# Forming P-Q on VectorE in 54 pair steps of an FNet and squared-ReLU kernel

## The chip, the cores and the metric

The kernel runs on one core of a Trainium2 chip. The metric is the device time of one execution in microseconds (us). Shown for the kernel before are three runs: 633.65, 633.65 and 635.58 us, median 633.65. One execution was profiled; all durations and waits below are of that one.

TensorE (PE in the profile) multiplies matrices into PSUM, ScalarE (ACT) and VectorE (DVE) work element by element, GpSimd (POOL) issues the loads here, and SyncE (SP) issues the stores. Each engine takes its instructions in the order in which the program gives them, and waits on semaphores for the others.

## What is computed

The input x is 8 batches of 3008 tokens with 256 features. The reference takes the real part of a Fourier transform over tokens and features, and passes each token through a two-layer network without biases:

```python
X = np.fft.fft(np.fft.fft(x, axis=1), axis=2).real     # 8 x 3008 x 256
x = X.reshape(24064, 256)
h = np.maximum(x @ w_in, 0.0)                          # w_in 256 x 2048
out = (h * h) @ w_out                                  # w_out 2048 x 256
```

## The kernel before

The transform is real in and real out, so tokens come in pairs k and S-k. The kernel holds, for a column (one token of a pair), the cosine part zc and the sine part zs, 128 features each. The feature transform is folded into the weights w_in once: gh[:, 0] takes zc, gh[:, 1] takes zs. With P = gh0' zc and Q = gh1' zs, the hidden layer of token k is P+Q and that of its partner P-Q. There is one exception: row 0 of gh1 and zs carries the term of the highest feature frequency, whose sign does not turn. gh[:, 2] is therefore -2 gh1 with row 0 set to 0 (`turn2`, `gh_turn`, L448), so that adding gh2' zs to P+Q gives the partner.

**Windows.** The columns of all batches are cut into 25 windows (`wins`): six of 240 to 512 columns, windows 6 to 23 of 512 columns, and a last one of 360. One window is eight pair steps (`for s0 in range(0, NST, ng)`), each for 256 of the 2048 hidden features (two halves a of 128):

- `pq`: four passes on TensorE (L684, L685) form P+Q of 256 features x 512 columns in a PSUM tile ph of two banks (ps_h has two such tiles).
- `square(s, 0)`: ScalarE evicts ph through Relu to h1 (L694, f16, three buffers), VectorE squares h1 into h2 (L696).
- `others(s)`: what else is due in this step, below.
- `turn`: two passes (L690) add gh2' zs to the same ph, which then holds P-Q.
- `square(s, 1)`: the same eviction and square for the partner. It writes the columns in reversed order.

**What lies in `others`.** First the jobs `at[s]`, then sixteen matmuls of the second layer of the window before (`ffn2_steps`, L596: h2 x wout16), every second step followed by the eviction osb (L611) and its output stores on SP's queue (L576); then `post[s]`; then matmuls of the transform (z, L478) for the next window, with their evictions on ScalarE (es L483, zc and zs L487) and combinations on VectorE (L494).

**Folds.** In some windows `at` brings the folding of a later batch on VectorE: d_even (L348, L349, L350) in step 0, n_cos (L358) in step 1, d_odd (fo, L353) in step 2, which also triggers the load of the next batch on GpSimd (L125, L130), n_sin (L361) in step 3, odds (od, L368) in step 4, nyq in `post[5]`, even (L379) in step 6, and back in step 7 (writes ev to DRAM and reads it back as rb on GpSimd's queue, L381, L389, L391). nyq is two small matmuls py on TensorE (L373, L374) that read od, and a copy back into od on VectorE (L375). Of the windows from 6 on, 8, 10, 13, 16 and 19 have folds. Windows 6, 9, 12, 15, 18 and 21 have the second part of a fold on VectorE instead ("late": xt L404, yt L415, steps 2 to 5).

The order on each engine is the order of the program text: `tc.manual_schedule()`; nothing is reordered. Tiles of one tag share their buffers in turn.

Of the kernel before, what the change touches and what calls it, by code (L numbers as in the profile page):

```python
# [8 lines left out]
F32 = mybir.dt.float32  # L9
F16 = mybir.dt.float16  # L10
I32 = mybir.dt.int32
AF = mybir.ActivationFunctionType
ALU = mybir.AluOpType

HS = 32.0
P = 128
# [3 lines left out]
def rev_dim(ap, i):  # L20

    dims = [list(d) for d in ap.ap]
    step, cnt = dims[i]
    dims[i] = [-step, cnt]
    return bass.AP(tensor=ap.tensor, offset=ap.offset + step * (cnt - 1), ap=dims)
# [3 lines left out]
def kernel(  # L29
# [14 lines left out]
    nc = tc.nc  # L44
    B, S, D = x.shape
    _, F = moe_w_in.shape
# [7 lines left out]
    NFC = F // P  # L54
    WN = 512

    FIRST = [240, 512, 376, 376, 512, 448]
    R23 = float(2.0 ** 23)

    RQ = (1, 3, 5, 0, 2, 4)  # L60

# [11 lines left out]
    wins = []  # L73
# [5 lines left out]
    NW = len(wins)  # L79

    def win_of(col):
        return max(w for w in range(NW) if wins[w][0] <= col) if col < TOT else NW
# [17 lines left out]
    const = ctx.enter_context(tc.tile_pool(name="const", bufs=1))  # L100
    tmp = ctx.enter_context(tc.tile_pool(name="tmp", bufs=2))
# [7 lines left out]
    drp = ctx.enter_context(tc.tile_pool(name="drp", bufs=2, space=bass.MemoryType.DRAM))  # L109
    ps_h = ctx.enter_context(tc.tile_pool(name="ps_h", bufs=2, space=bass.MemoryType.PSUM))  # L110
    ps_o = ctx.enter_context(tc.tile_pool(name="ps_o", bufs=2, space=bass.MemoryType.PSUM))
# [56 lines left out]
    perm = [const.tile([P, P], F16, name=f"perm{i}") for i in range(2)]  # L168
# [3 lines left out]
    nc.gpsimd.memset(idx["c"][0:2, :], P - 3)  # L172
    idx["f"] = iota([P, 1], [[1, 1]], -1, 1, "idx_f")
    nc.gpsimd.memset(idx["f"][0:1, :], 0)
    w16 = [const.tile([P, 2, F // 2], F16, name=f"w16_{i}") for i in range(2)]
    for i in range(2):
        nc.gpsimd.dma_start(out=w16[i], in_=moe_w_in[:, i * F // 2 : (i + 1) * F // 2].rearrange("(c p) f -> p c f", p=P))
    wout16 = const.tile([P, NFC, D], F16, name="wout16")
# [2 lines left out]
    def small(shape, name):  # L181
        return const.tile(shape, F32, name=name)
# [22 lines left out]
    def table_steps(e):  # L205
# [19 lines left out]
        def args(h):  # L225
            t = st["t", h] = tmp.tile([P, 3, NE], F32, name="t", tag="tt")
            for j in range(nr):
                r = row(h, j)
                if e == 0:
                    nc.scalar.activation(t[:, j, 0:n], st["kf"], AF.Copy, bias=R23, scale=vs[:, r : r + 1])  # L230
                else:
                    nc.vector.tensor_scalar(out=t[:, j, 0:n], in0=st["kf"], scalar1=vs[:, r : r + 1], scalar2=R23, op0=ALU.mult, op1=ALU.add)

        def turns(h):
            t = st["t", h]
            nc.vector.tensor_scalar(out=t[:, 0:nr, 0:n], in0=t[:, 0:nr, 0:n], scalar1=-R23, scalar2=-float(S), op0=ALU.add, op1=ALU.mult)

# [44 lines left out]
    at = const.tile([P, 2, P + 1], F32, name="at")  # L282
    for c in range(2):
        nc.scalar.activation(at[:, c, :], drow, AF.Copy, bias=R23, scale=dvs[:, c : c + 1])
    nc.vector.tensor_scalar(out=at, in0=at, scalar1=-R23, scalar2=-float(D), op0=ALU.add, op1=ALU.mult)
    for c in range(2):
# [141 lines left out]
    gh = const.tile([P, 3, F], F16, name="gh")  # L428
# [17 lines left out]
    def gh_turn(cc):  # L446
        f0 = cc * 512
        nc.vector.tensor_scalar(out=gh[:, 2, f0 : f0 + 512], in0=gh[:, 1, f0 : f0 + 512], scalar1=turn2[:, 0:1], scalar2=None, op0=ALU.mult)  # L448
# [3 lines left out]
    def zwin(w):  # L452
        if w not in zc:
            zc[w] = zp.tile([P, WN], F16, name="zc", tag="zc")
            zs[w] = zp.tile([P, WN], F16, name="zs", tag="zs")
        return zc[w], zs[w]
# [101 lines left out]
    for cc in range(1, F // 512):  # L558
        gh_turn(cc)

    def store(osb, p0, g0, m, minus, eng=nc.sync):

        for b, k0, kstep, n, c0 in runs:
            il, ih = max(g0, c0) - c0, min(g0 + m, c0 + n) - 1 - c0
            if minus and k0 in (0, H):
                il = max(il, 1)
            cnt = ih - il + 1
            if cnt <= 0:
                continue
            if minus:  # L570
                lo = p0 + (m - 1) - (c0 + ih - g0)
                row = b * S + S - (k0 + kstep * ih)
            else:
                lo = p0 + c0 + il - g0
                row = b * S + k0 + kstep * il
            eng.dma_start(  # L576
                out=bass.AP(tensor=out.tensor, offset=out.offset + row * D, ap=[[kstep * D, cnt], [1, D]]),
                in_=osb[lo : lo + cnt, :])
# [51 lines left out]
    def fold_jobs(i):  # L630
        f = folds[i] = fold_steps(i)
        return [f["d_even"], f["n_cos"], f["d_odd"], f["n_sin"], f["odds"], f["nyq"], f["even"], f["back"]]

    fold_at, late_at = {}, {}
    for i in range(2, B):
        fold_at[win_of(col_of[i, 0]) - 2] = i
        late_at[win_of(col_of[i, 1]) - 2] = i
    NST = NFC // 2
    old = None
    for w in range(NW):  # L640
        g0, wn = wins[w]
        h2 = h2p.tile([P, NFC, 2 * WN], F16, name="h2", tag="h2")
        zcw, zsw = zwin(w)

        lo, hi = 0, NST - 1
        at = [[] for _ in range(NST)]
        post = [[] for _ in range(NST)]
        if w == 0:
            at[2] = [f0s["even"], f0s["back"]]
        elif w == 1:  # L650
            fj = fold_jobs(1)
            at = [[f] for f in fj[0:5]] + [[], [], []]
            post[5] = fj[5:6]
            lo, hi = 6, 7
        elif w == 2:
            te = table_steps(1)
            at = [[folds[1]["even"], lambda: te["freq"](), lambda: te["args"](0)], [lambda: te["turns"](0)], [lambda: te["mods"](0)],
                  [lambda: te["absm"](0)], [lambda: te["sins"](0)], [lambda: te["coss"](0)], [], [lambda: te["weigh"]()]]
            for st in range(4):
                at[st + 3] = at[st + 3] + f0s["late"][st : st + 1]  # L660
            at[7].append(folds[1]["back"])
        elif w in fold_at:
            fj = fold_jobs(fold_at[w])
            at = [[f] for f in fj[0:5]] + [[], fj[6:7], fj[7:8]]
            post[5] = fj[5:6]
        elif w == win_of(col_of[1, 1]) - 1:
            for st in range(4):
                at[st] = folds[1]["late"][st : st + 1]
            lo = 4
        if w in late_at:  # L670
            for st in range(4):
                at[st + 2] = at[st + 2] + folds[late_at[w]]["late"][st : st + 1]
        zj, zl = [], []
        for u in need[w + 1]:
            zu = z_steps(u)
            zj += [(zu, 0, 0), (zu, 1, 0), (zu, 0, 1), (zu, 1, 1)]
        f2 = ffn2_steps(*old) if old else []
        phs = {}

        def pq(s):  # L680
            ph = phs[s] = ps_h.tile([P, 2, 512], F32, name="ph", tag="psh")
            for a in range(2):
                f0 = (2 * s + a) * P
                nc.tensor.matmul(ph[:, a, 0:wn], gh[:, 0, f0 : f0 + P], zcw[:, 0:wn], start=True, stop=False)  # L684
                nc.tensor.matmul(ph[:, a, 0:wn], gh[:, 1, f0 : f0 + P], zsw[:, 0:wn], start=False, stop=True)  # L685

        def turn(s):
            for a in range(2):
                f0 = (2 * s + a) * P
                nc.tensor.matmul(phs[s][:, a, 0:wn], gh[:, 2, f0 : f0 + P], zsw[:, 0:wn], start=False, stop=True, skip_group_check=True)  # L690

        def square(s, sg):
            h1 = h1p.tile([P, 2, 512], F16, name="h1", tag="h1")
            nc.scalar.activation(h1[:, :, 0:wn], phs[s][:, :, 0:wn], AF.Relu)  # L694
            hv = rev_dim(h1[:, :, 0:wn], 2) if sg else h1[:, :, 0:wn]
            nc.vector.tensor_tensor(h2[:, 2 * s : 2 * s + 2, sg * wn : (sg + 1) * wn], hv, hv, op=ALU.mult)  # L696

        def others(s):
            for j in at[s]:
                j()  # L700
            for j in spread(f2, s, NST):
                j()
            for j in post[s]:
                j()
            if s == lo:
                zl[:] = [j for zu, part, h in zj for j in zu(part, h)]
            if s >= lo:
                for j in spread(zl, s - lo, hi - lo) if s < hi else []:
                    j()


        ng = 2 if w == 0 or wins[w - 1][1] < 384 < wn else 1
        for s0 in range(0, NST, ng):
            ss = range(s0, s0 + ng)
            for s in ss:
                pq(s)
            for s in ss:
                square(s, 0)
            others(s0)
            for s in ss:  # L720
                turn(s)
            for s in ss:
                square(s, 1)
            for s in ss[1:]:
                others(s)
        old = (w, h2)
    for j in ffn2_steps(*old, tail=True):
        j()
# [30 lines left out]
```

## Time and profile before

| what | value |
|---|---|
| median of the runs | 633.65 us |
| profiled execution, span from first to last instruction | 632.0 us |
| TensorE busy | 615.9 us, 97% |
| ScalarE busy | 457.4 us, 72% |
| VectorE busy | 369.5 us, 58% |
| GpSimd busy | 76.5 us, 12% |
| granted TensorE clock, share of full speed | 1.000 |
| second-layer matmuls L596 | 3024, 51% of the chain of waits |
| passes L684, L685, L690 | 400 each, 12% of the chain each |
| a pair step of a window of 512, no z matmuls | 3.04 us |

The span is what the profiler saw between the first and the last instruction; the run's time is 1.65 us more at the median. "Busy" of TensorE counts a matmul until it has drained, so neighbours overlap, and its mean duration (379 ns for a pass of 512 columns) is longer than the distance from one to the next. The distance is what counts for time; it is read from the timeline. In lines of groups and of the timeline, out<-in names the tiles, and what stands in brackets is the idle time of the engine before the instruction with what ended it.

### The profile page before, as it was taken

How to read it: one execution, taken by the hardware profiler on the slowest of the kernel's cores; microseconds unless marked ns; L12 is line 12 of the kernel's file. 1: busy time of each engine (PE TensorE's matmuls, PEld its weight loads, DVE VectorE, ACT ScalarE, POOL GpSimd, SP SyncE). 2: the span in 40 equal slices, each digit the busy share in tenths (PEclk: the TensorE clock that was granted, in tenths of full speed). 3: DMA queues.
4: the chain of work that ended last, by engine and by line, in shares of the span. 5: the costliest groups of instructions: out<-in, count | busy, mean ns of one | idle time of the engine just before them, and what ended most of it. 6: DMA issues, size and time to landing. Idle time of an engine off the chain costs nothing.

```text
span 632.0 us, 11586 instructions
## 1 busy us (share of the span) xinstructions
PE 615.9 (97%) x4548; PEld 439.1 (69%) x4548; DVE 369.5 (58%) x604; ACT 457.4 (72%) x610; POOL 76.5 (12%) x125
## 2 busy tenths in 40 slices
PE   5899999999999999999999999999999999999997
PEld 2457776776777767767777677777677776777786
DVE  7887656765457557645576455854557555454430
ACT  7787778777777677767777777777777777777662
POOL 5352200022002200220011100030000200000000
PEclk9999999999999999999999999999999999999999
DMA  8936211172112711631127211262111311111112
GB/s 146 211 82 127 85 34 34 50 164 78 36 43 58 184 46 42 144 97 35 51 44 160 74 52 39 59 151 73 40 31 55 111 34 47 38 46 35 49 54 65
DMA packets 36525, 47.52 MB, mean 75 GB/s; under 512 B 4216, under 2 KB 30328, under 8 KB 36472
## 3 DMA queue, kind: packets, MB, share of 16 engines
q0 software_dynamic: 9344, 22.14, 17.6%
q1 hardware_dynamic: 26899, 24.44, 12.7%
q8 instruction: 35, 0.57, 0.4%
q10 hardware_dynamic: 228, 0.21, 0.1%
q14 instruction: 19, 0.15, 0.1%
HBM read 33.63 MB, written 27.84 MB: 97 GB/s over the span
## 4 chain that ended last, share of the span: by engine, by line
PE 93%; DVE 3%; ACT 2%; issue 1%; POOL 0%; ACTq 0%; POOLq 0%; DVEq 0%
PE po L596 51%; PE ph L684 12%; PE ph L685 12%; PE ph L690 12%; PE pz L478 4%; ACT h L694 1%; PE pw L301 1%; DVE h L696 1%; PE pg L436 0%; ACT cos L259 0%; DVE fe L349 0%; DVE fo L353 0%; ACT sin L248 0%; ACT gh L440 0%; DVE od L368 0%
## 5 line engine op out<-in xcount | busy, mean ns | idle before, releaser
L694 ACT ACTIVATE h<-ph 128x1024 f16<-128x1024 f32 (+4 forms) x400 | 368.4, 974 | 80.0 <-PE ph L690 72.1
L696 DVE TENSOR_TENSOR h<-h 128x1024 f16<-128x1024 f16 (+4 forms) x400 | 262.4, 660 | 231.6 <-ACT h L694 228.2
L596 PE MATMUL po<-wout,h 128*128 128x256 f16 (+1 forms) x3024 | 361.6, 273 | 0.0
L596 PEld LDWEIGHTS <-h 128*128 128x128 f16 (+1 forms) x3024 | 296.8, 98 | 71.3
L684 PE MATMUL ph<-zc,gh 128*128 128x512 f16 (+4 forms) x400 | 145.9, 366 | 1.1 <-ACT h L694 0.8
L685 PE MATMUL ph<-zs,gh 128*128 128x512 f16 (+4 forms) x400 | 145.9, 366 | 0.4 <-ACT zs L487 0.4
L690 PE MATMUL ph<-zs,gh 128*128 128x512 f16 (+4 forms) x400 | 112.8, 366 | 2.0 <-ACT h L694 1.5
L611 ACT ACTIVATE osb<-po 128x512 f32<-128x512 f32 (+3 forms) x95 | 54.9, 582 | 57.4 <-PE po L596 52.4
L685 PEld LDWEIGHTS <-gh 128*128 128x128 f16 x400 | 39.1, 98 | 43.8 <-issue 2.5
L684 PEld LDWEIGHTS <-gh 128*128 128x128 f16 x400 | 39.0, 98 | 41.8 <-issue 0.5
L690 PEld LDWEIGHTS <-gh 128*128 128x128 f16 x400 | 37.2, 97 | 12.7 <-issue 4.3
L421 POOL COPY xt<-xt 128x2 f16<-128x2 f16 x16 | 2.5, 186 | 173.2 <-DVE xt L404 173.2
L130 POOL DMA_INDIRECT xo<-in_x_dram,idx_r x15 | 22.1, 1471 | 4.6 <-issue 4.6
L125 POOL DMA_DIRECT2D xo<-in_x_dram x8 | 6.0, 751 | 109.8 <-DVE fo L353 109.8
L483 ACT ACTIVATE es<-pz 128x376 f32<-128x376 f32 (+1 forms) x32 | 15.4, 481 | 5.3 <-PE pz L478 5.2
L391 POOL DMA_INDIRECT rb<-scr,idx_r x16 | 18.5, 1158 | 4.9 <-issue 4.9
L487 ACT ACTIVATE zs<-pz 128x376 f16<-128x376 f32 (+23 forms) x27 | 8.5, 358 | 9.9 <-PE pz L478 9.9
L349 DVE TENSOR_TENSOR fe<-xo 128x3072 f16<-128x3072 f16 x8 | 14.3, 1786 | 1.6 <-DMA xo<-in_x_dram,idx_r 1.3
L353 DVE TENSOR_TENSOR fo<-xo 128x3072 f16<-128x3072 f16 x8 | 14.2, 1779 | 0.0
L494 DVE SCALAR_TENSOR_TENSOR zc<-es,pz 128x376 f16<-128x376 f32 (+20 forms) x26 | 9.4, 392 | 7.2 <-ACT zc L487 7.0
L301 PE MATMUL pw<-spn 128*128 128x384 f16 x30 | 8.2, 448 | 5.2 <-DVE spn L290 5.2
L389 POOL DMA_DIRECT2D rb<-scr x16 | 8.8, 551 | 33.4 <-DMA scr<-ev 33.0
(106 smaller groups left out, 220.4 us busy)
## 6 DMA issues: line engine op xcount, KB each, us to landing
out_dram<-osb SPq DMA_DIRECT2D x77, 128.0 KB
xo<-in_x_dram POOLq DMA_DIRECT2D x7, 768.0 KB, 7.0
scr<-ev POOLq DMA_DIRECT2D x8, 390.0 KB, 4.4
rb<-scr POOLq DMA_DIRECT2D x16, 130.0 KB, 5.1
out_dram<-osb SPq DMA_DIRECT2D x12, 94.0 KB
w<-in_moe_w_in_dram POOLq DMA_DIRECT2D x2, 512.0 KB, 10.0
wout<-in_moe_w_out_dram POOLq DMA_DIRECT2D x1, 1024.0 KB, 14.5
out_dram<-osb SPq DMA_DIRECT2D x8, 75.0 KB
```

The source lines that it names most:

```text
L130: nc.gpsimd.indirect_dma_start(out=flat(q), out_offset=None, in_=bass.AP(tensor=x.tensor, offset=0, ap=[[XW, B * S * D // XW], [1, XW]]), ...
L301: nc.tensor.matmul(pw[:, 0 : 3 * P], spn[:, 0, 0, :], spn.rearrange("p c r d -> p (c r d)")[:, 0 : 3 * P], start=True, stop=True)
L391: nc.gpsimd.indirect_dma_start(out=rb[:, q].rearrange("p r d -> p (r d)"), out_offset=None, in_=bass.AP(tensor=src.tensor, offset=src.offs ...
L478: nc.tensor.matmul(ps[:, o0:o1], lhs, tab, start=(h == 0 and k == 0), stop=last, skip_group_check=True)
L483: nc.scalar.activation(es[:, 0:n], ps[:, 0:n], AF.Copy, bias=0.0, scale=1.0)
L596: nc.tensor.matmul(po[0:m, j * D : (j + 1) * D], h2[:, fc, q : q + m], wout16[:, fc, :], start=(fc == 0), stop=(fc == NFC - 1))
L611: nc.scalar.activation(osb[0:mm].rearrange("p s d -> p (s d)")[:, lo:hi], po[0:mm, lo:hi], AF.Copy, bias=0.0, scale=HS * HS)
L684: nc.tensor.matmul(ph[:, a, 0:wn], gh[:, 0, f0 : f0 + P], zcw[:, 0:wn], start=True, stop=False)
L685: nc.tensor.matmul(ph[:, a, 0:wn], gh[:, 1, f0 : f0 + P], zsw[:, 0:wn], start=False, stop=True)
L690: nc.tensor.matmul(phs[s][:, a, 0:wn], gh[:, 2, f0 : f0 + P], zsw[:, 0:wn], start=False, stop=True, skip_group_check=True)
L694: nc.scalar.activation(h1[:, :, 0:wn], phs[s][:, :, 0:wn], AF.Relu)
L696: nc.vector.tensor_tensor(h2[:, 2 * s : 2 * s + 2, sg * wn : (sg + 1) * wn], hv, hv, op=ALU.mult)
```

## The change

In windows 6 to 23, steps 1, 3 and 5 (18 x 3 = 54 pair steps) do not run the third TensorE pass. `half_q` forms Q alone in ph; ScalarE copies -2Q to the tile sn (f16). TensorE then does `others`, and `half_p` adds P to ph; ScalarE copies P+Q to hd. VectorE adds the two to get P-Q, written reversed beside P+Q in hd, takes the max with 0 over both (2048 elements) and squares both into h2 with one instruction.

For the term whose sign does not turn, -2Q has to be put right: twice row 0 of gh1, times row 0 of zs, is added. `row_weights` (once, in window 3) gets 2 gh1[0] as a value per partition by 16 one-column matmuls; `row_spread` (at the end of the window before) writes row 0 of zs to DRAM (zr) and reads it back into all 128 partitions (eb), two DMAs on SP's queue. Two scalings on VectorE make the term in the second half of sn, and a sum adds it to -2Q.

sn takes the two buffers of the weights w16, which are no longer read; hd the tags tt and tm of the tables, two buffers each; eb the tag kf.

```diff
+    MANY, FEW = (1, 3, 5), (1, 3, 5)
...
-    w16 = [const.tile([P, 2, F // 2], F16, name=f"w16_{i}") for i in range(2)]
+    w16 = [const.tile([P, 2, F // 2], F16, name=f"w16_{i}", tag=f"w16_{i}") for i in range(2)]
...
+    wv = small([P, NFC], "wv")
+
+    def row_weights():
+
+        pv = ps_o.tile([P, 512], F32, name="pv", tag="po")
+        for fc in range(NFC):
+            nc.tensor.matmul(pv[:, fc : fc + 1], gh[:, 1, fc * P : (fc + 1) * P], perm[0][:, P - 1 : P], start=True, stop=True)
+        nc.vector.tensor_scalar(out=wv, in0=pv[:, 0:NFC], scalar1=2.0, scalar2=None, op0=ALU.mult)
+
+    eb = {}
+
+    def row_spread(w):
+
+        wn = wins[w][1]
+        zr = drp.tile([1, WN], F16, name="zr", tag="zr")
+        nc.sync.dma_start(out=zr[0:1, 0:wn], in_=zwin(w)[1][0:1, 0:wn])
+        t = eb[w] = tmp.tile([P, WN], F16, name="eb", tag="kf")
+        src = zr[0:1, 0:wn]
+        nc.sync.dma_start(out=t[:, 0:wn], in_=bass.AP(tensor=src.tensor, offset=src.offset, ap=[[0, P], [1, wn]]))
...
+    def halved(w):
+
+        if wins[w][1] < WN or w < 6:
+            return ()
+        return FEW if w in fold_at else MANY
+
+    ROT = [0]
...
+        if w == 3:
+            at[0].append(row_weights)
...
+        two = halved(w)
+        sns, hds = {}, {}
+
+        def half_q(s):
+            ph = phs[s] = ps_h.tile([P, 2, 512], F32, name="ph", tag="psh")
+            for a in range(2):
+                f0 = (2 * s + a) * P
+                nc.tensor.matmul(ph[:, a, 0:wn], gh[:, 1, f0 : f0 + P], zsw[:, 0:wn], start=True, stop=True)
+            i = ROT[0] % 2
+            sn = sns[s] = const.tile([P, 2, 2, WN], F16, name=f"sn{i}", tag=f"w16_{i}")
+            nc.scalar.activation(sn[:, 0, :, 0:wn], ph[:, :, 0:wn], AF.Copy, bias=0.0, scale=-2.0)
+            for a in range(2):
+                nc.vector.tensor_scalar(out=sn[:, 1, a, 0:wn], in0=eb[w][:, 0:wn], scalar1=wv[:, 2 * s + a : 2 * s + a + 1], scalar2=None, op0=ALU.mult)
+            nc.vector.tensor_tensor(sn[:, 0, :, 0:wn], sn[:, 0, :, 0:wn], sn[:, 1, :, 0:wn], op=ALU.add)
+
+        def half_p(s):
+            ph, sn = phs[s], sns[s]
+            for a in range(2):
+                f0 = (2 * s + a) * P
+                nc.tensor.matmul(ph[:, a, 0:wn], gh[:, 0, f0 : f0 + P], zcw[:, 0:wn], start=False, stop=True, skip_group_check=True)
+            hd = tmp.tile([P, 2, 2 * WN], F16, name="hd", tag=("tt", "tm")[ROT[0] % 2])
+            ROT[0] += 1
+            nc.scalar.activation(hd[:, :, 0:wn], ph[:, :, 0:wn], AF.Copy, bias=0.0, scale=1.0)
+            nc.vector.tensor_tensor(rev_dim(hd[:, :, wn : 2 * wn], 2), hd[:, :, 0:wn], sn[:, 0, :, 0:wn], op=ALU.add)
+            nc.vector.tensor_scalar(out=hd, in0=hd, scalar1=0.0, scalar2=None, op0=ALU.max)
+            nc.vector.tensor_tensor(h2[:, 2 * s : 2 * s + 2, :], hd, hd, op=ALU.mult)
...
+            if s0 in two:
+                half_q(s0)
+                others(s0)
+                half_p(s0)
+                continue
...
+        if w + 1 < NW and halved(w + 1):
+            row_spread(w + 1)
```

## The prediction

> **What bounds the kernel now.** I read the page first: the busy times, then the chain of waits.
>
> ```profile
> PE 615.9 (97%) x4548; PEld 439.1 (69%) x4548; DVE 369.5 (58%) x604; ACT 457.4 (72%) x610; POOL 76.5 (12%) x125
> ...
> PE 93%; DVE 3%; ACT 2%; issue 1%; POOL 0%; ACTq 0%; POOLq 0%; DVEq 0%
> ```
>
> TensorE is 97% busy and is 93% of the chain that ended last. To see that it is really issuing and not only "busy", I went to the timeline of a quiet stretch (window 15):
>
> ```profile
> 377.77 0.59 PE L690 MATMUL ph<-zs,gh 128*128 128x512 f16 x2
> ...
> 378.20 0.38 PE L684 MATMUL ph<-zc,gh 128*128 128x512 f16 x1
> 378.20 0.10 PEld L685 LDWEIGHTS <-gh 128*128 128x128 f16 x1
> 378.40 1.94 ACT L694 ACTIVATE h<-ph 128x1024 f16<-128x1024 f32 x2 [1.04 <-PE ph L690]
> ```
>
> Two third passes (L690) start at 377.77 and the next step starts at 378.20: 0.43 us for two. Pair steps follow each other every 3.04 us there, which is 6 passes of 0.215 us and 16 second-layer matmuls (1.75 us). ScalarE starts 0.20 us after a step begins and has slack. So a pass taken out of TensorE is time, as long as nobody else becomes late.
>
> VectorE decides that. By stage (windows 13, 14 and 15 of the kernel, each 8 pair steps):
>
> ```profile
> 342.80:369.10 26.30, 26.30 (x190) 18.41 (x189) 12.36 (x20) 19.15 (x27) 3.07 (x4) 1.00 0.33 89
> 369.00:393.40 24.40, 24.40 (x178) 17.23 (x176) 12.97 (x20) 17.53 (x21) 0.63 (x4) 1.00 0.14 44
> 317.30:342.80 25.50, 25.50 (x199) 18.43 (x198) 19.05 (x27) 19.15 (x27) 4.89 (x5) 1.00 0.45 92
> ```
>
> The third busy column is VectorE: 12 to 13 us in most windows, but 19.05 of 25.5 us in window 13, where a batch is folded. The 58% of the page hides that. Windows 8, 10, 13, 16 and 19 are such fold windows among the 18 that the change touches (6 to 23).
>
> **What is removed.** 54 steps lose two passes: 54 x 0.43 = **-23.2 us**. Weight loads go with them and lie under matmuls.
>
> **TensorE, added.** Sixteen one-column matmuls in window 3 (row_weights). The nearest rows, two such matmuls (L373, L374), start 0.03 us apart; the second-layer ones 0.11. So 0.5 to 1.8 us, I take **+1.0**, nothing beside it.
>
> **ScalarE.** Two evictions of 1024 elements before, two after; a Copy (L440) takes 1024 ns, the Relu (L694) 1026. Equal. But in a half step only 0.43 us of passes stand before the 1.75 us of other matmuls, so P's pass can start at 2.18 us. ScalarE first finishes the eviction of the step before and then -2Q: by the row above the two end at 0.20 + 1.94 = 2.14, and TensorE follows a ScalarE release in some 0.06 us (24.50 after 24.44, window 0). 2.20 against 2.18: 0.02 x 54 = **+1.1**; upper end 0.1 each, 5 us.
>
> **VectorE, per half step.** Out: two squares (L696, 692 ns; back to back they start 0.605 apart). In, from the nearest rows: two scalings of 512 f16 (L448, 341 ns, in a series 0.28 apart): 0.62. Two sums of 1024 f16: 0.69 each. The max on 2048: L448 (512: 341 ns) and L265 (377: 314 ns) rise by 0.20 ns an element, so 0.65; at the slope of the two-input rows (692 ns for 1024, 550 for 752) it would be 1.23. The square of 2048: 692 + 1024 x 0.52 = 1.23. A dependent instruction starts 0.04 after the one before it (L365 behind L358), an independent one 0.085 before its end. Together **3.96 us** where 1.21 stood. The second sum writes reversed; rows with reversed reads (half of L696) cost no more, so I take 0.69, upper end 1.2.
>
> In a quiet window that is 12.4 + 3 x 2.75 = 20.6 us of VectorE in 23 to 25 us. Fits: h2 is read a window later, and the last square of step 7 has until 2.4 us into the next window.
>
> **Fold windows are where the stall arises.** TensorE itself waits for VectorE there: the Nyquist matmul py (L373, step 5) reads od, the last of a chain of folds, and everything behind it on TensorE, P's passes first, waits too. Window 13 has both ends:
>
> ```profile
> 333.15 0.97 DVE L368 TENSOR_TENSOR od<-ab 128x1548 f16<-128x1548 f16 x1
> ```
>
> ```profile
> 335.93 0.17 PE L373 MATMUL py<-od,perm 128*128 128x1 f16 x1
> ```
>
> od is ready at 334.12, py comes at 335.93: 1.81 us to spare (1.84 in window 8). Now py comes earlier by three missing pairs (steps 1, 3 and Q before P in 5), 1.29 us: 17.37 us after the window's start (317.27) instead of 18.66. And od comes later. From the first half step's scalings: half step with n_cos between (3.96 + 0.75 = 4.71), square 0.605, fo 1.695, square 0.605, half step with n_sin 4.71, square 0.605, od 0.97: 13.9 us. The scalings can start when the folds of step 0 and square (0,1) are done, 5.5 us into the window, and when eb has landed.
>
> **eb** is two DMAs one after the other on SP's queue, behind the last output stores, and is new. The last osb of a window is evicted 0.37 us into the next (343.20 against 342.83), two to four stores take up to 1.55 us to issue (381.63 to 383.18), so zr goes out at about 1.2 to 1.9. A store's first bytes move 0.8 us after its issue (DMA view from 381.6: 8 empty slices of 0.1 us); the kernel's last store, issued 627.90, was landed 2.5 us later. Reads of scr by rb land after 2.4 to 5.2 us. So eb lands between 1.2 + 0.8 + 2.4 = 4.4 and 1.9 + 2.6 + 5.2 = 9.7. I take 6, near the low end, for a row of 1 KB is far less than these transfers. SP's later stores wait behind it; osb has three buffers, some 15 us of cover.
>
> So od at 6 + 13.9 = 19.9 against 17.4: **2.5 us** in windows 10, 13, 16, 19. In window 8 the steps have no z matmuls and py comes at 17.82 - 1.29 = 16.53: 3.4. Sum **+13.4**. Before this change the same wait stands once in the trace, in window 1, where VectorE is full:
>
> ```profile
> PE py L373 <- DVE od L368: 1.0, 1, 1.0
> ```
>
> While TensorE waits VectorE catches up: the squares and z columns behind od take 7 us, TensorE's rest of the window over 7.2, so no second stall is due.
>
> **Sum.** 632.0 - 23.2 + 1.0 + 1.1 + 13.4 = 624.3 us of span. The median of the runs is 633.65, 1.65 above this span: **626.0 us**.
>
> **Rivals.**
> 1. *All of it is kept.* VectorE keeps ahead of py, because gaps that I count as lost close up. 632.0 - 23.2 + 2.1 + 1.65 = 612.6. For it: VectorE is idle 2.3 us before od in window 13. Against: I have spent them. 15%.
> 2. *Slower: eb comes late.* Each us costs five (five fold windows). The gain without stalls is 21.1 us; 13.4 is spent at 6 us, so at 6 + 7.7/5 = 7.5 us nothing is left. Beyond that the late windows without z (12, 15, 18, 21) also miss the square of step 7. At 9.7: 13.4 + 18.5 + 4 x 2.2 = 41 lost, 653. For it: two landings in series, behind stores of odd row counts. Against: tiny transfers. 20%.
> 3. *VectorE is dearer.* The max at 1.23, the reversed write at 1.2: 1.1 more per half step, two of them before od, five windows: +11, 637. One of the two alone: 631.5. 13%.
> 4. *GpSimd gets in the way.* In fold windows it issues the next batch's loads (L130, about 1 us each, four or five) beside VectorE. In the trace a square that met L391 at 350.79 took 0.75 instead of 0.69: 0.06 us each. If whole instructions were held, two before od would cost 2 x 1.0 x 5 = +10, 636. [...] 7%.
>
> That the change does not take the passes out I rule out: its program has 92 matmul and load pairs fewer on TensorE (108 less, 16 more).
>
> **Chances.** The forecast has 45%. The measurement tells 0.3% (1.9 us) from no change. Faster: nearly all of the forecast, rival 1, a third of 3 and 4: **0.62**; same: **0.13**; slower: **0.25**. The range takes in rival 1 at its low end, and eb up to about 8.5 us at its high end (626 + 5 x 2.5 + 4): 612 to 642.
>
> **What would show it.** Right: the gap py <- od of 2 to 4 us in five windows, half steps of 2.6 us, ScalarE as busy as before, VectorE near 515 us. Wrong: waits of the scalings for eb over 2 us, max over 1 us, P's passes waiting for ScalarE by more than 0.1 us, or stalls at a window's start.

## The result and the profile after

The changed kernel takes 665.39 us (median of 4 runs, 662.47 to 669.04) beside 633.74 us of the kernel before on the same chip (4 runs, 633.65 to 635.58): a ratio of 1.0498, 95% interval 1.0459 to 1.0537. It is 5% slower, 39 us from the forecast and outside its range. The profiled execution has a span of 660.5 us, 28.5 more than before.

Parts 1 and 4 of its page, to be read beside the first fence of the prediction (busy time of the engines; shares of the chain that ended last), and the row of the granted clock in tenths over 40 slices:

```profile
PE 606.5 (92%) x4456; PEld 432.0 (65%) x4456; DVE 487.7 (74%) x821; ACT 459.6 (70%) x610; POOL 78.8 (12%) x125
...
PEclk9999999999998999898998999999998899999999
...
PE 50%; DVE 25%; DMA 13%; issue 5%; ACT 5%; POOL 1%; SPq 1%; DVEq 0%; ACTq 0%; POOLq 0%
```

TensorE has its 92 matmuls fewer, yet it carries only 50% of the chain, where it carried 93%. VectorE has 25% now, and transfers 13%. Digits of 8 in the clock's row are new, for before the change all 40 are 9: the mean granted clock of the execution is 0.976 where it was 1.000.

The arithmetic that was added has the forecast durations. Groups of the changed lines (x count, then busy us, mean ns of one, then the idle time before them and what ended it):

```profile
L752 ACT ACTIVATE hd<-ph 128x1024 f16<-128x1024 f32 x54 | 55.5, 1027 | 23.4 <-PE ph L749 23.3
L755 DVE TENSOR_TENSOR h<-hd 128x2048 f16<-128x2048 f16 x54 | 66.2, 1225 | 1.8
...
L753 DVE TENSOR_TENSOR hd<-hd,sn 128x1024 f16<-128x1024 f16 x54 | 37.2, 688 | 4.8 <-ACT hd L752 2.6
...
L754 DVE TENSOR_SCALAR hd<-hd 128x2048 f16<-128x2048 f16 x54 | 37.5, 694 | 1.9
```

The max (L754) is 0.69 us, not 1.23, and the sum with the reversed write (L753) is 0.69 us, like the sum without (L743, 0.69). One group stands out by its right side:

```profile
L742 DVE TENSOR_SCALAR sn<-eb,wv 128x512 f16<-128x512 f16 x108 | 33.1, 348 | 61.4 <-DMA eb<-zr 61.4
```

VectorE stood still for 61.4 us in all before the scalings, waiting for eb. The waits in order of engines (us in total, times, longest), of which the last is of SP's queue:

```profile
DVE sn L742 <- DMA eb<-zr: 61.4, 14, 10.0
```

```profile
PE py L375 <- DVE od L370: 24.0, 6, 9.9
PE ph L749 <- ACT sn L740: 7.1, 3, 3.8
...
PE po L618 <- DVE h L728: 4.2, 4, 1.3
PE ph L717 <- DVE zs L496: 3.3, 3, 1.7
```

```profile
SPq L581 <- DMA zr<-zs: 57.0, 18, 6.7
```

So SP waits for zr to land in DRAM before it may issue eb (57.0 us in 18 windows); VectorE waits for eb in 14 of 18 windows; TensorE waits for VectorE (24.0 us at py, 7.5 more at po and zs) and, behind VectorE's lateness, for ScalarE (7.1).

**Where the time went, by window.** From the starts of the first pass of each step, window length after minus before, in us:

| windows | after minus before |
|---|---|
| 6, 9, 12, 14, 22 (no stall) | -1.30, -1.29, -1.23, -1.29, -1.30 |
| 8, 10, 13, 16, 19 (folds) | +6.29, +4.45, +3.41, +3.31, +10.02 |
| 7, 15, 18, 21 (step 0 waits for zs or for squares of the window before) | +0.10, +0.03, +0.45, +0.44 |
| 11, 23 (P's passes wait in step 5) | +4.30, +2.44 |
| 17, 20 (0.6 and 0.3 lost in step 5) | -0.69, -1.00 |
| all 18 | +27.1 |

The five in which TensorE does not stall gain 1.23 to 1.30 us, three pairs of passes at 0.43, although VectorE waited 1.6 to 5.7 us for eb in them. All else is stalls and what follows them. The remaining 1.4 of the 28.5 us is lost in the last window, whose po waits for squares of window 23.

**Why eb comes late.** SP's queue in window 11, which starts at 274.95, and in window 10, which starts at 244.94 (start, duration, operation):

```profile
275.35 1.39 SPq L598 DMA_DIRECT2D out_dram<-osb  x4
276.83 3.51 SPq L578 DMA_DIRECT2D zr<-zs  x1
287.08 0.35 SPq L581 DMA_DIRECT2D eb<-zr  x1
```

```profile
245.33 0.83 SPq L598 DMA_DIRECT2D out_dram<-osb  x2
246.95 0.24 SPq L578 DMA_DIRECT2D zr<-zs  x1
248.05 0.33 SPq L581 DMA_DIRECT2D eb<-zr  x1
```

From zr to eb it is 1.10 us in window 10 and 10.25 us in window 11. The two stores ahead of zr have 128 rows each in window 10; the four in window 11 have 11, 117, 44 and 83. The rate of all transfers in the DMA view of window 11, 275 to 291 us in slices of 0.4 us, shows what moves in between:

```profile
GB/s 329 351 67 74 220 182 18 36 13 64 26 23 23 140 221 273 88 23 189 179 18 151 210 26 26 23 23 31 8 0 0 0 23 95 110 172 207 279 100 36
```

Before eb is issued (slice 31) there are five slices at 23 to 31 GB/s (24 to 28), and three at 23 to 26 earlier (11 to 13), where full slices have 200 to 350. A row is 1 KB, so 83 rows take some 3.5 us at 24 GB/s. In the five slices (284.2 to 286.2 us) the busy share of the 16 DMA engines is 0.07, where the first two slices (275.0 to 275.8) have 0.89. Window 23 has the same without any load of GpSimd beside it: its four stores have 75, 53, 15 and 113 rows, zr is issued at 597.78 and eb at 605.96, and the rate (597.8 to 605.8 us in slices of 0.2 us) is that of one row every 0.04 us in most slices from 599.4 on:

```profile
GB/s 82 21 15 10 10 10 10 20 26 26 26 20 26 21 26 26 26 20 26 26 26 20 26 26 102 26 26 26 20 26 26 20 26 26 26 20 26 26 0 0
```

From 599.6 to 605.4 SP's queue moves 140 packets there and keeps 6.8% of the 16 engines busy, 1.1 engines. That the rows of one store then go one by one over a single engine is an estimate from these shares; no run shows what decides it.

Odd row counts, which rival 2 named, are not needed for it: behind 106, 22, 46 and 82 rows (window 20) zr to eb is 6.1 us, behind two stores of 128 (windows 10, 15, 18 and 21) 1.1 to 1.4. Something else is in the way too. In windows 9, 11, 14, 17 and 20, each right behind a fold, 0.4 to 0.9 MB of GpSimd's loads are moved between zr's issue and eb's. In window 17 (437.4 to 444.2 us; q0 is GpSimd's queue, q1 SP's; packets, MB, share of the 16 engines) they fill most of the 6.7 us, and none of SP's rows is moved in the first 2.3:

```profile
q0 software_dynamic: 279, 0.92, 61.3%
q1 hardware_dynamic: 288, 0.26, 11.4%
```

No run took these loads away, so the two are not priced apart.

After eb's issue another 3.0 us pass in window 11 until the scalings start (287.08 to 290.10). Over all 18 windows zr to eb takes 1.1 to 10.2 us (median 3.0), and eb to its use, where VectorE waits for it, 2.9 to 3.5.

**The clock.** TensorE in window 13, whose od came late:

```profile
349.13 0.16 PE L375 MATMUL py<-od,perm 128*128 128x1 f16 x1 [3.02 <-DVE od L370]
...
350.38 0.63 PE L716 MATMUL ph<-zc,gh 128*128 128x512 f16 x1
350.81 0.63 PE L717 MATMUL ph<-zs,gh 128*128 128x512 f16 x1
351.23 0.63 PE L716 MATMUL ph<-zc,gh 128*128 128x512 f16 x1
...
354.52 0.38 PE L716 MATMUL ph<-zc,gh 128*128 128x512 f16 x1
354.73 0.38 PE L717 MATMUL ph<-zs,gh 128*128 128x512 f16 x1
```

After 3.02 us of standing still the passes start 0.43 us apart; from 354.52 on it is 0.21 again. The same in the table by stages (span, then busy PE, PEld, VectorE, ScalarE, GpSimd, the granted clock, DMA) for windows 13, 14 and 15, beside the prediction's rows for them:

```profile
328.60:357.50 28.90, 25.88 (x193) 18.37 (x192) 27.46 (x42) 19.35 (x27) 4.28 (x5) 0.94 0.40 83
357.60:382.50 24.90, 24.90 (x183) 17.77 (x182) 15.45 (x27) 19.05 (x27) 3.06 (x4) 1.00 0.40 102
382.60:406.80 24.20, 23.22 (x171) 16.43 (x170) 22.02 (x38) 17.50 (x21) 1.24 (x4) 1.00 0.16 49
```

Over the whole span a mean of 0.976 means some 32 us at half clock (2 x 0.024 x 660.5), at most 16 us lost.

### The profile page after: what moved, and what is told of

Same layout as the page of the kernel before. It is cut to its first block, busy times and chain, and to the rows that moved or that the text cites. A ratio compares the mean times of both kernels' runs of the same rounds, so it can differ in the third digit from the quotient of the medians.

```text
span 660.5 us, 11678 instructions
## 1 busy us (share of the span) xinstructions
PE 606.5 (92%) x4456; PEld 432.0 (65%) x4456; DVE 487.7 (74%) x821; ACT 459.6 (70%) x610; POOL 78.8 (12%) x125
## 4 chain that ended last, share of the span: by engine, by line
PE 50%; DVE 25%; DMA 13%; issue 5%; ACT 5%; POOL 1%; SPq 1%; DVEq 0%; ACTq 0%; POOLq 0%
PE po L618 29%; DMA zr<-zs 7%; DVE h L728 6%; PE ph L717 5%; PE ph L716 5%; PE ph L722 5%; DMA eb<-zr 4%; DVE h L755 4%; DVE hd L754 3%; DVE hd L753 3%; ACT h L726 3%; DVE sn L743 2%; PE ph L749 2%; DVE sn L742 2%; PE pz L480 2%
## 5 line engine op out<-in xcount | busy, mean ns | idle before, releaser
L726 ACT ACTIVATE h<-ph 128x1024 f16<-128x1024 f32 (+4 forms) x292 | 270.9, 957 | 105.0 <-PE ph L722 65.2
L728 DVE TENSOR_TENSOR h<-h 128x1024 f16<-128x1024 f16 (+4 forms) x292 | 183.4, 644 | 78.0 <-ACT h L726 74.5
L717 PE MATMUL ph<-zs,gh 128*128 128x512 f16 (+4 forms) x292 | 107.7, 371 | 3.7 <-DVE zs L496 3.3
L716 PE MATMUL ph<-zc,gh 128*128 128x512 f16 (+4 forms) x292 | 107.8, 371 | 1.1 <-ACT h L726 0.8
L722 PE MATMUL ph<-zs,gh 128*128 128x512 f16 (+4 forms) x292 | 80.7, 361 | 2.5 <-ACT h L726 1.7
L742 DVE TENSOR_SCALAR sn<-eb,wv 128x512 f16<-128x512 f16 x108 | 33.1, 348 | 61.4 <-DMA eb<-zr 61.4
L752 ACT ACTIVATE hd<-ph 128x1024 f16<-128x1024 f32 x54 | 55.5, 1027 | 23.4 <-PE ph L749 23.3
L755 DVE TENSOR_TENSOR h<-hd 128x2048 f16<-128x2048 f16 x54 | 66.2, 1225 | 1.8
L740 ACT ACTIVATE sn<-ph 128x1024 f16<-128x1024 f32 x54 | 55.0, 1018 | 0.0
L743 DVE TENSOR_TENSOR sn<-sn 128x1024 f16<-128x1024 f16 x54 | 37.4, 692 | 5.6
L753 DVE TENSOR_TENSOR hd<-hd,sn 128x1024 f16<-128x1024 f16 x54 | 37.2, 688 | 4.8 <-ACT hd L752 2.6
L754 DVE TENSOR_SCALAR hd<-hd 128x2048 f16<-128x2048 f16 x54 | 37.5, 694 | 1.9
L722 PEld LDWEIGHTS <-gh 128*128 128x128 f16 x292 | 27.2, 98 | 11.4 <-issue 5.3
```

Of the source, the lines that this page charges most:

```text
L740: nc.scalar.activation(sn[:, 0, :, 0:wn], ph[:, :, 0:wn], AF.Copy, bias=0.0, scale=-2.0)
L752: nc.scalar.activation(hd[:, :, 0:wn], ph[:, :, 0:wn], AF.Copy, bias=0.0, scale=1.0)
L753: nc.vector.tensor_tensor(rev_dim(hd[:, :, wn : 2 * wn], 2), hd[:, :, 0:wn], sn[:, 0, :, 0:wn], op=ALU.add)
L754: nc.vector.tensor_scalar(out=hd, in0=hd, scalar1=0.0, scalar2=None, op0=ALU.max)
L755: nc.vector.tensor_tensor(h2[:, 2 * s : 2 * s + 2, :], hd, hd, op=ALU.mult)
```

## The experiments

The theory after the result: the half steps cost what was forecast; eb is late because its two DMAs stand behind the stores on SP's queue; what is lost is that lateness, with the half clock that follows a stall. Rivals: VectorE is too full whatever eb does (A); two transfers in series are late by themselves, on any queue (B).

### Without the DMAs of 17 windows: e1_eb_once

All windows use the eb of window 6, so 17 windows leave out the right values of the correction; everything else is as in the change.

```diff
-            row_spread(w + 1)
+            if 6 in eb:
+                eb[w + 1] = eb[6]
+            else:
+                row_spread(w + 1)
```

> Left out: the two DMAs of every window but the first halved one; eb of window 6 serves all windows, so the correction of the term whose sign does not turn is that of other columns. VectorE's work is the same. Theory (two causes add up: eb lands late, 61 us of VectorE waits; and VectorE's backlog ahead of py in the five fold windows): the first cause is gone. 13 windows keep their gain of 1.3 us, the fold windows lose 3.3 us each as windows 13 and 16 did with almost no eb wait: 630 to 637 us. Rival A (VectorE's added work alone is what costs; its waits for eb only fill time that it would have idled): 655 to 665 us.

Measured: 626.21 us beside 635.29, ratio 0.9877 (0.9849 to 0.9905), span 624.2 us, clock 0.997. Its waits:

```profile
PE py L375 <- DVE od L370: 12.2, 6, 2.9
```

```profile
DVE sn L742 <- DMA eb<-zr: 2.8, 1, 2.8
```

Windows without a fold gain 1.26 to 1.30 us each (window 7, still behind window 6's eb, 0.06). Fold windows are +1.79, +0.95, +0.95, +0.91 and +2.57. So eb alone stands between the forecast and the change, 36.3 us of span; A falls as the cause of the slowdown, though its five py stalls remain. The time is below the 630 to 637 us expected: the fold windows were priced at 3.3 us each, as in windows 13 and 16 of the change, where half clock followed the stall. Here only window 19 has half clock behind it.

### zr on another queue: e2_zr_own_queue

```diff
-        nc.sync.dma_start(out=zr[0:1, 0:wn], in_=zwin(w)[1][0:1, 0:wn])
+        nc.scalar.dma_start(out=zr[0:1, 0:wn], in_=zwin(w)[1][0:1, 0:wn])
```

> Only zr goes out on ScalarE's queue instead of SP's; eb stays on SP's. Theory (zr is late because it stands behind output stores of odd row counts in the same queue; it took 1.1 to 6.7 us until eb could be issued, 3.2 in the mean): zr lands after about 1.2 us, VectorE's waits for eb fall from 61 to about 25 us, 645 to 655 us. Rival B (the landing of a small DMA simply takes that long): waits and time as with the change, 660 to 669 us.

Measured: 639.08 us, ratio 1.0080 (1.0054 to 1.0106), better than the theory expected. SP's wait for zr falls from 57.0 to a quarter:

```profile
SPq L581 <- DMA zr<-zs: 14.8, 9, 3.6
```

```profile
DVE sn L742 <- DMA eb<-zr: 36.8, 10, 8.3
```

Two things changed at once: zr goes out 0.2 to 0.3 us into most windows (mostly 1.3 to 2.0 in the change), and from its issue to that of eb it is 1.1 to 4.7 us (1.1 to 10.2). The lateness of zr is thus for the most part that of its place on SP's queue. Part of it moves to eb, which still stands there, so that the waits for eb fell less than expected (to 36.8, not 25): where the scalings wait, it comes 2.9 to 9.4 us after its issue (2.9 to 3.5 in the change).

### The DMAs one step earlier: e3_spread_earlier

`row_spread` is called before step 7 of the window before instead of after it.

```diff
         for s0 in range(0, NST, ng):
             ss = range(s0, s0 + ng)
+            if s0 == NST - 1 and w + 1 < NW and halved(w + 1):
+                row_spread(w + 1)
...
-        if w + 1 < NW and halved(w + 1):
-            row_spread(w + 1)
         old = (w, h2)
```

> The two DMAs are issued one pair step earlier (ahead of step 7 and its stores), nothing else changes. Theory: eb lands about 3 us earlier and is less often behind stores; VectorE's waits for it fall from 61 to about 15 us, 637 to 648 us. Rival A: 655 to 665 us.

Measured: 635.53 us, ratio 1.0007 (0.9992 to 1.0022): no change against before, 30 us less than the change, and just below the range expected. zr is as late behind its queue (SP waits 50.9 us for it, 57.0 in the change), but 3 us of lead hide most of it:

```profile
DVE sn L742 <- DMA eb<-zr: 18.8, 7, 6.5
```

### eb without any DMA: e4_eb_by_tensore

A matmul with a selector (ones in row 0) spreads row 0 of zs over 128 partitions, ScalarE copies it out, in step 0 of the window itself.

```diff
+    sel = const.tile([P, P], F16, name="sel")
+    nc.gpsimd.memset(sel, 0.0)
+    nc.gpsimd.memset(sel[0:1, :], 1.0)
...
-        zr = drp.tile([1, WN], F16, name="zr", tag="zr")
-        nc.sync.dma_start(out=zr[0:1, 0:wn], in_=zwin(w)[1][0:1, 0:wn])
+        pe = ps_o.tile([P, 512], F32, name="pe", tag="po")
+        nc.tensor.matmul(pe, sel, zwin(w)[1], start=True, stop=True)
         t = eb[w] = tmp.tile([P, WN], F16, name="eb", tag="kf")
-        src = zr[0:1, 0:wn]
-        nc.sync.dma_start(out=t[:, 0:wn], in_=bass.AP(tensor=src.tensor, offset=src.offset, ap=[[0, P], [1, wn]]))
+        nc.scalar.activation(t, pe, AF.Copy, bias=0.0, scale=1.0)
...
+        if halved(w):
+            at[0] = at[0] + [lambda w=w: row_spread(w)]
```

> No DMAs: one TensorE pass per window with a matrix whose row 0 is ones spreads row 0 of zs over the partitions, ScalarE copies it to eb (18 passes of 0.215 us on TensorE, 18 copies of 0.6 us on ScalarE). Theory: no eb waits; like the run that loads eb once, 3.9 us more: 634 to 641 us. Rival A: 659 to 669 us.

Measured: 628.61 us, ratio 0.9904 (0.9886 to 0.9923), span 625.3 us. Each of 17 windows pays 0.20 to 0.22 us at step 0 and none waits for eb. These windows, as far as they have no fold, gain 1.05 to 1.08 us (window 6, which pays nothing, 1.29); fold windows lose 0.96 to 1.01, and window 8 3.46, with 1.50 of it in the step behind its stall. The time is below the 634 to 641 us expected, as with e1.

```profile
PE py L375 <- DVE od L370: 11.3, 6, 2.7
```

### The fold windows spared, or lightened: f1_folds_spared, f2_folds_1_6

From here on with eb by TensorE. What is left of the loss should be the half steps ahead of od in fold windows.

```diff
-    MANY, FEW = (1, 3, 5), (1, 3, 5)
+    MANY, FEW = (1, 3, 5), ()
```

> eb by TensorE, and no half steps in windows with folds (39 half steps instead of 54). Theory (what is left of the loss is VectorE's backlog ahead of py in the fold windows, 2.0 to 4.5 us each): these five windows go back to their old length, the other 13 keep 1.07 us each (1.29 less the spreading pass): 632.0 - 13.9 = 618 us of span, 620 us. Rival C (the loss is spread over all half steps, by ScalarE or memory being busier): taking 15 half steps out gives back 15 x 0.43 us of gain, 634 us or more.

```diff
-    MANY, FEW = (1, 3, 5), (1, 3, 5)
+    MANY, FEW = (1, 3, 5), (1, 6)
```

> eb by TensorE, and in windows with folds two half steps, 1 and 6, so that only one of them stands ahead of od. Theory: py waits no more (od at about 16.8 us after the window's start, py at 18.4), each fold window gains 0.86 - 0.22 us: 632.0 - 13.9 - 3.2 = 615 us of span, 616.5 us. Rival C: 630 us or more.

Measured: f1 620.05 us, ratio 0.9768 (0.9752 to 0.9785); f2 616.91 us, ratio 0.9734 (0.9706 to 0.9761). Both as expected; f2 is the fastest kernel of this study, with a clock of 1.000. In f2 the fold windows gain 0.63 to 0.65 us (two half steps less the 0.22), and of the py waits only that of window 1 is left, which was there before the change:

```profile
PE py L375 <- DVE od L370: 1.0, 1, 1.0
```

One half step ahead of od fits; two do not.

### py later: f3_py_in_step_7

As e4, but py is due two steps later in halved fold windows, so that it no longer asks for od early.

```diff
-            post[5] = fj[5:6]
+            post[7 if halved(w) else 5] = fj[5:6]
```

> eb by TensorE, all 54 half steps, but in fold windows the two py matmuls stand in step 7 instead of step 5. If py is the only place where VectorE's backlog reaches TensorE, all 18 windows gain 1.07 us: 613 us of span, 614 us. Theory: the backlog stays (about 2 us at the window's end) and shows at the next place, the sine columns zs that the next window's first passes read, 1 to 1.5 us in each of five windows: 619 to 622 us.

Measured: 630.68 us, ratio 0.9930 (0.9908 to 0.9952), 2 us slower than e4 rather than faster. The five fold windows gain 1.06 to 1.08 us, and the windows behind them lose 2.7 to 4.4 in step 0:

```profile
PE po L619 <- DVE od L377: 11.9, 5, 2.5
```

The backlog shows at the next thing that TensorE needs from VectorE, as expected, but the price was too low (619 to 622 us) and the place is another than named: the PSUM buffer that py shares with the second layer's po, freed by VectorE's small copy L377, which stands behind the late half steps, folds and squares. The granted clock falls to a half behind two of the five waits, in windows 9 and 11, which lose 4.4 and 4.3; the other three lose 2.7.

### Matmuls in the gap: f4_fill_before_py

The change itself, with 14 matmuls of 384 columns into py's buffer ahead of py in the fold windows. They add 2.3 us of work where TensorE would stand still; nothing reads them.

```diff
             py = ps_o.tile([P, 512], F32, name="py", tag="po")
+            for k in range(FILL[0]):
+                nc.tensor.matmul(py[:, 0:384], gh[:, 0, 0:P], gh[:, 0, 0:384], start=True, stop=True)
...
+        FILL[0] = 14 if two else 0
```

> The change as it is (with the two DMAs), and in the fold windows 14 matmuls of 384 columns (about 2.2 us) ahead of py that need nothing and whose result is overwritten. py itself can come no earlier. Theory (after TensorE has stood still for 2 us or more it runs at half clock for about 3.4 us, which costs 1 to 1.8 us in step 6 of each fold window): where the wait was 2 to 3 us (windows 10, 13, 16) TensorE does not stand still for long, the clock stays at 1.0, 1 to 1.7 us saved each: 3 to 6 us less than the change. Rival D (step 6 is longer for another reason, for instance ScalarE catching up): no less, or 2 us more where the fillers outlast the wait.

Measured: 664.77 us, ratio 1.0476 (1.0459 to 1.0494). For the total it is inconclusive, since other windows are longer than in the change: 11, 14 and 17 by 1.5 to 1.9 us, because eb came 1.5 to 2.0 us later, and 19 and 23 by 1.5, with eb within 0.3 us of where it was but more half clock behind the wait. But windows 10, 13 and 16 are 1.7, 1.5 and 1.9 us shorter. Window 13, with od as late as in the change (349.37 against 349.13):

```profile
346.17 2.44 PE L377 MATMUL py<-gh 128*128 128x384 f16 x14
349.37 0.16 PE L378 MATMUL py<-od,perm 128*128 128x1 f16 x1 [0.76 <-DVE od L371]
...
350.05 0.38 PE L719 MATMUL ph<-zc,gh 128*128 128x512 f16 x1
350.27 0.38 PE L720 MATMUL ph<-zs,gh 128*128 128x512 f16 x1
```

The passes behind it start 0.215 us apart instead of 0.43. So in these windows the half clock comes from TensorE's standing still, and costs 1.5 to 1.7 us beyond the wait itself (of the 1.9 of window 16, 0.2 is an od that came earlier).

### Both DMAs on GpSimd's queue: g1_both_gpsimd, g2_gpsimd_folds_1_6

```diff
-        nc.sync.dma_start(out=zr[0:1, 0:wn], in_=zwin(w)[1][0:1, 0:wn])
+        nc.gpsimd.dma_start(out=zr[0:1, 0:wn], in_=zwin(w)[1][0:1, 0:wn])
...
-        nc.sync.dma_start(out=t[:, 0:wn], in_=bass.AP(tensor=src.tensor, offset=src.offset, ap=[[0, P], [1, wn]]))
+        nc.gpsimd.dma_start(out=t[:, 0:wn], in_=bass.AP(tensor=src.tensor, offset=src.offset, ap=[[0, P], [1, wn]]))
```

> The change, with both DMAs of row_spread (zr and eb) issued by GpSimd on its own queue, where no output store stands before them. In the run with only zr on another queue, the scalings waited 36.8 us for eb (61.4 in the change). Theory (the lateness is the queue of stores, and the two landings in series take about 5 us by themselves): nothing is left in the windows without a fold but small waits, so they gain 1.2 to 1.3 us each; in the fold windows eb comes about 6 us after the window's start, as the prediction had it, with stalls of 2 to 3.5 us: waits for eb under 15 us, span 622 to 630, time 624 to 632. Rival (two landings in series are late by themselves, whatever the queue): eb still 8 us or more after the window's start, waits over 30 us, time 636 or more. A second rival (GpSimd's issues stand behind its loads and copies of a fold, or are slow beside VectorE): the fold windows alone are late, with waits for eb of 5 us or more there, time 632 to 640.

g2 has the same edit, and FEW = (1, 6) as f2.

> As the run before it, and in the five fold windows the half steps are 1 and 6 only, so that just one stands before od. The same choice of steps with eb made by TensorE took 616.9, with one matmul of 0.22 us in each of 17 windows. Theory (DMAs on a free queue are in time, and cost TensorE nothing): 17 x 0.22 = 3.7 us less, 613 to 614. Rival (eb is late still by 2 us or more in some windows): 616 or more, with waits of py or of a window's first step.

Measured: g1 681.04 us beside 634.66, ratio 1.0714 (1.0671 to 1.0757); g2 669.58 us, ratio 1.0519 (1.0473 to 1.0566). Both theory and prices fell. In g1 VectorE waits 71.4 us for eb, though the transfers themselves are not slow: without stores in front zr lands 1.6 to 5.9 us after its issue (median 2.4) and eb 3.1 to 6.3 (median 3.3). The issue is late. GpSimd's order around the start of window 11 of g1 (284.98):

```profile
284.97 0.60 POOL L383 DMA_DIRECT2D scr<-ev  x1 [9.57 <-DVE ev L381]
291.25 1.10 POOL L391 DMA_DIRECT2D rb<-scr  x2 [5.67 <-DMA scr<-ev]
...
294.94 0.56 POOL L578 DMA_DIRECT2D zr<-zs  x1
299.66 0.58 POOL L581 DMA_DIRECT2D eb<-zr  x1 [4.16 <-DMA zr<-zs]
```

zr stands behind the fold's own store and loads (scr, rb), which wait for VectorE and for each other, and goes out 10 us into the window. In window 17 eb was waited for 18.4 us. This is the rival of GpSimd's order, but its price was far too low, and it falls on the windows behind folds (6, 9, 11, 14, 17 and 20) rather than on the fold windows. B is right in part: by the two medians two transfers take 5.7 us in series here, where the scalings could start about 5 us into a window. By the median the change is hardly slower (3.0 from zr to eb, and some 3 more). What it has beyond that are the long ones, up to 10.2 us, and e2 shows that zr's place on SP's queue makes most of them.

## Why the prediction was wrong

**The step that failed is eb**: "So eb lands between ... 4.4 and ... 9.7. I take 6, near the low end, for a row of 1 KB is far less than these transfers." Size was not what counted; what was moved ahead of it was. Measured in the change, zr goes out 1.3 to 5.0 us into a window, takes 1.1 to 10.2 us until SP may issue eb, and eb about 3 us more. Only windows 10, 13 and 16 of the fold windows had eb near 6 (6.4 and 6.2 in 13 and 16; 7.3 at most in 10); 8 had it at 7.8 and 19 at 13.3, and outside the folds window 11 had it at 15.2. The upper bound of 9.7 was passed in six windows. The rows that bounded it (an unhurried last store, the loads rb on GpSimd's queue) held no small transfer that stood behind stores of uneven row counts on its own queue.

**That cost 36.3 us** (660.5 of span against 624.2 in e1). The longer waits of TensorE account for 26: py 24.0 against 12.2, P's passes 7.1, po 4.2, zs 3.3 against 1.1, and 0.7 in L722. The remaining 10 is put down to the half clock, which by the means 0.976 and 0.997 could be up to 14.

**The half clock was missing.** The prediction gave a stall its own length. In window 13 the stall itself was as worked out: eb at 6.4, py 3.02 us late, by the working 2.5 + 0.4 = 2.9. But the window is 3.41 us longer, not 3.02 - 1.29 = 1.73; f4 shows that 1.5 of that was the clock.

**The other steps, by e1, where eb is there:**
- Passes removed, 54 x 0.43: right, 0.42 to 0.44 in each of them.
- row_weights, +1.0: 0.17 us, by which window 3 is longer in every run.
- The hand-off of sn, +1.1: nothing. Quiet windows gain the full 1.29.
- VectorE's 3.96 us per half step: by the groups 211 us for 54, 3.91 each; 4.10 from one to the next in a full queue. Rival 3 is wrong. VectorE's total, forecast near 515, is 487.7: 14 of the 27 us are the removed squares (79 us, not 54 x 1.21 = 65); the rest these rows do not explain.
- The stall at py, +13.4: in e1 the fold windows stand at +7.17 in sum where they would have gained 6.45, so 13.6. Its waits are 2.91 us in window 8 and 2.04 to 2.09 in the others; the working gives 2.9 and 2.0 if the scalings start at 5.5 us, when the folds of step 0 let them, instead of at 6. The waits are 11.2 of the 13.6; 1.6 more than in its neighbours is lost in window 19, at half clock.
- "No second stall is due" held behind the fold windows, in e1 and in the change: windows 9, 11, 14, 17 and 20 lose nothing in step 0. But in the change windows 7, 10, 15, 18 and 21 lose 1.3 to 1.8 us there. VectorE, late with eb in the window before them, had not finished zs (7, 10) or the last squares (15, 18, 21; rival 2 had these).

e1's span is 624.2 where 624.3 was forecast. Some of that is luck: with eb at hand the working gives 624.3 - 5 x 0.5 = 621.8; 1.9 of it did not come (row_weights, sn), and 2.7 at the folds, 1.2 in window 7 (behind window 6's eb) and some 0.4 elsewhere came that were not in it.

**The rivals.** Rival 2 (20%) came true as a mechanism, but its price was too low: it stopped at 653, with eb at 9.7 and mostly in the five fold windows, while in the change the lateness goes beyond that and the half clock adds to it. Rival 1 is wrong: the stalls at py are there even when eb is (e1, e4). Rival 4, GpSimd in the way of VectorE, is hardly seen: in the change the eight scalings that run beside an instruction of GpSimd take 345 to 393 ns, the others 347 in the mean: 0.05 us more at most, where its +10 took 1.0 for an instruction held.

## What to carry to other kernels

A small transfer that others wait for must be priced by what stands before it on its queue and by the number of round trips in series, not by its bytes: here 1 KB took 1.1 us from zr's issue to eb's behind two stores of 128 rows and 8.2 behind four of 15 to 113 (windows 10 and 23), and two landings in series 5.7 by the medians of g1. If a compute engine can make the value cheaply, that can beat the DMAs even on the engine that bounds the kernel (one matmul of 0.22 us a window here, and 37 us less than with two DMAs). A stall of TensorE can cost more than its length, since 2 to 3 us of standing still can be followed by 3.4 us or more at half clock. Work that is moved to a second engine fits or not per stage: three half steps fit everywhere but in the fold windows, and there only one fits ahead of the result that TensorE waits for.

## What the hardware showed that was not expected

- **The same stall sometimes halves the clock and sometimes does not.** In e1 TensorE stood still 2.09 us in window 13, 2.04 in window 16 and 2.04 in window 19. Only after the last did the clock fall:

```profile
480.54:483.95 3.41, 1.37 (x16) 1.10 (x14) 3.38 (x5) 1.55 (x3) 0.00 (x0) 1.00 0.14 41
483.95:487.36 3.41, 3.41 (x13) 1.57 (x12) 3.26 (x8) 1.58 (x2) 0.00 (x0) 0.50 0.13 41
...
330.35:333.76 3.41, 2.34 (x19) 1.76 (x18) 3.34 (x6) 2.74 (x5) 0.27 (x1) 1.00 1.05 199
333.76:337.18 3.42, 2.40 (x19) 1.61 (x19) 3.32 (x8) 1.51 (x2) 0.00 (x0) 1.00 0.95 202
405.44:408.86 3.42, 1.78 (x17) 1.45 (x15) 3.35 (x5) 2.18 (x3) 0.00 (x0) 1.00 0.78 136
408.86:412.27 3.41, 3.02 (x25) 2.15 (x25) 3.30 (x8) 1.94 (x2) 0.00 (x0) 1.00 0.17 44
```

  The rows are stretches of e1 around the stalls of windows 19 (the first two), 13 and 16. The first busy column is TensorE, and the third last column is the granted clock. The stretches are cut on a grid that the clock's record shows: in the change the half-clock stretches start at 208.96, 266.99, 297.71, 348.91, 427.41 and 505.92 us, all a whole number of steps of 3.413 us apart, and each lasts one, two or three steps. The stall of window 19 lies within one step, which has 2.04 us of idle time, and the next step is at half clock. The stalls of windows 13 and 16 are cut by a boundary into 1.07 and 1.02 us, and 1.64 and 0.39. In the twelve traces, from 25 us on and by the profile's busy times, every step at full clock with at least 2.04 us of idle time (30 of them) is followed by half clock, none with at most 1.97 us is, and none lies between. So in these traces how much of a stall falls into one step decides whether half clock follows.
- **A short DMA can hold its issuer.** The issue of zr in window 11 took 3.51 us on SP's queue, where it mostly takes 0.24.
- **A reversed write is free** on VectorE at this shape: 688 ns (L753) beside 692 ns (L743).

What stays open is how much of zr's lateness is the row counts of the stores ahead and how much, behind folds, GpSimd's loads. No run had the same stores with 128 rows each, and none went without the loads.
